# Tokens in halves, split feed-forward chunks and a new order table in a linear-attention and max-out kernel

## The chip, the cores and the metric

The kernel runs on one core of one Trainium2 chip. The metric is the device time of one execution in microseconds. A core has five engines with queues of their own: TensorE (PE; PEld is its weight load), VectorE (DVE), ScalarE (ACT), GpSimd (POOL) and SyncE (SP), which here only issues transfers. Engines work their queues in order and wait for each other by semaphores.

## The reference

q, k and v have shape 8 x 8 x 576 x 64 (batch, heads, tokens, channels), all inputs are float32.

```python
def phi(x):
    proj = np.einsum('bhsd,df->bhsf', x, w_phi)                       # 128 features
    proj = proj - np.max(np.abs(proj), axis=-1, keepdims=True)
    return np.concatenate([np.exp(proj), np.exp(-proj)], axis=-1)
q_p, k_p = phi(q), phi(k)
kv = np.einsum('bhsf,bhsd->bhfd', k_p, v)
z = np.sum(k_p, axis=2)
num = np.einsum('bhsf,bhfd->bhsd', q_p, kv)
den = np.einsum('bhsf,bhf->bhs', q_p, z)[..., None] + 1e-06
x = (num / den).transpose(0, 2, 1, 3).reshape(B * S, H * D)           # 4608 x 512
h = np.maximum(np.maximum(x @ w1, x @ w2), x @ w3)                    # 4608 x 768
out = h @ w_out                                                       # 4608 x 512
```

## The kernel before

The attention runs in 16 units of four heads (unit u is half of batch u // 2). A unit has 18 tiles of 128 tokens: 16 for the first 512 tokens of its four heads and two for the last 64 tokens of each (its tail, which for q is loaded apart, L383). The steps of a unit, with the names that the tables show:

- load q, k, v (`q_raw`, `k_raw`, `v_raw`; for units 0 to 3 q and k are cast on the way by POOL's transfers, L451 and L466, except unit 0's k, L458, which is cast by L462; the tail of q is cast by L487). Casts of later units are on POOL (L510).
- transpose q and k to `qkT`: by PE for units 0 to 3 (L495, copied out by L500), by a transposing transfer for the others (L514).
- project with `w_phi` (L536), take the largest absolute value of each token on DVE (`mk`, `mq`, L548), exponentiate on ACT (`Ek` L545, `Eq` L613 after a second projection L607), scale v by `em` on POOL (`vab`, L566), and multiply into `kvps` (L587), copied to `kv_sb` (L593).
- the quotient: `psn` (L638) holds the two products with exp(proj) and exp(-proj); DVE forms y = psn[0] * sq (L641, the first sums), adds psn[1] (L644) and takes the reciprocal of the denominator (L646); POOL or DVE multiplies (`x_sb`, L648). Each of these works on one or two heads with five tiles of 65 columns.
- transpose to `xT`: by PE for units 0 to 5 (L658, copied by L661), by a transposing transfer for the others (L665).

Every two units make a batch, and its first 512 tokens a feed-forward chunk; the last 64 tokens of all eight batches make a ninth, chunk 8. The maximum over three products is rewritten: w2 and w3 have w1 subtracted (L763, on POOL and DVE), so a chunk needs only x(w2-w1) and x(w3-w1) (`ups`, L688), ReLU (`hT`, L696 or L698), a maximum (L694), and the product with w_out (L721) beside x(w1 w_out) (L716), whose weights are made once (`pwT` L775, `pm` L789). The results are copied out (`osb`, L729) and stored (L736). The weights are loaded by four transfers on POOL (L421).

The order of the work on every engine is written out by hand: `PLAN` is a table of entries such as `1176G@10.0` (node 1176, on POOL, with the time for which it was planned). `plan` reads it and gives each node its engine, its buffers and its place; the engines then run their instructions in the table's order. The eight banks of PSUM and the work buffers are given out in the table too. A `gate` (L479) is a copy of one element on DVE into a `v_raw` buffer, after which that unit's v may be loaded; the load then waits at the head of SP's queue, and all later loads behind it.

Of the kernel before, what the change touches and what calls it, by code (L numbers as in the profile page):

```python
# [8 lines left out]
FP32 = mybir.dt.float32  # L9
# [27 lines left out]
EARLY = 2  # L37
WARM = 28.0
# [46 lines left out]
4G0@0.4 6S0@0.4 2S@1.0 0G@1.2 5G@1.8 8S@2.2 93G1@2.7 10S0@2.8 92G@3.5 7D@3.7 11S0@4.1 3D@4.2 13T0@4.3 253G2@4.3  # L85
14D0@5.0 252G@5.2 9A@5.3 24T001200@5.8 19T34@6.0 27D@6.3 21A@6.5 12G@6.6 15T5@6.7 96G@6.8 23D@6.9 26A@7.0 17T6@7.2
178S0@7.2 16D@7.5 20A@7.5 177G0@7.5 25A@8.0 18D@8.1 29T70@8.2 22D@8.3 176G@8.4 39T35@8.5 63T6200@8.6 30A@8.7 28D@8.9
65A@9.2 1173G@9.2 94D@9.5 42D@9.6 34T41@9.7 31A@9.7 95S@9.8 33D@10.0 1176G@10.0 41A@10.2 36A@10.5 43D@10.6 101T7@10.7
1174G@10.8 32D@10.9 40A@10.9 99T3@11.1 64A@11.2 97T5@11.5 102D1@11.5 1175G@11.6 67A@11.7 37D@11.7 68T0@12.1 58T67@12.2
401S0@12.2 44A0@12.2 98D@12.3 66A@12.4 46G0@12.5 69A@12.9 100D@13.0 108T112511@13.1 35A@13.2 38D@13.6 62A@13.6  # L90
113T31@13.8 256G@13.9 181G@14.1 70A@14.1 112D@14.2 45G@14.3 48A@14.4 103T40@14.6 109A@14.6 117D@14.8 257T2@14.9
104A@15.1 111D@15.4 261T3@15.6 61A@15.6 329S0@15.6 47G@15.7 49G@15.9 262D2@16.0 105A@16.1 107D@16.2 52T073@16.4
59A@16.5 106D@16.8 110A@17.0 50G@17.2 116D@17.4 60A@17.5 118T45@17.7 259T0@18.0 53A@18.0 122D@18.1 128A1@18.2
114A@18.4 123T67@18.5 51G@18.6 121D@18.7 400S@18.8 130G1@18.8 54A@18.9 152T411@18.9 115A@19.1 126D@19.4 154A@19.6
127D@19.7 55T31@19.7 124A@19.9 260D@20.0 119A@20.1 129G@20.1 182T6@20.4 56A@20.6 258D@20.7 125A@20.8 186T0@20.9
71A0@21.1 147T37@21.3 187D0@21.3 132A@21.3 57D@21.5 153A@21.5 72T20@21.6 135G@21.7 183D@21.7 120A@21.8 131G@21.9
75T14@22.0 133G@22.2 149A@22.3 73D0@22.3 184T5@22.4 76D@22.8 155A1@22.8 328S@22.9 151A@23.0 136T162@23.0 74D@23.2
148A@23.4 134G@23.5 77D@23.6 83T10@23.7 150A@23.9 138D@24.0 142T34@24.2 185D@24.2 137A@24.4 80T27@24.6 145A@24.6
# [194 lines left out]
def kernel(  # L293
# [562 lines left out]
```

## Time and profile before

| what | value |
|---|---|
| median of 3 runs | 294.62 us (292.95 to 296.05) |
| the profiled execution | 292.23 us, with a span of 290.1 us |
| PE busy | 270.6 us, 93% of the span, 3502 matmuls |
| DVE busy | 230.2 us, 79%, 458 instructions |
| ACT busy | 204.7 us, 71%, 493 instructions |
| POOL busy | 157.7 us, 54%, 163 instructions |
| moved by transfers | 49.92 MB in 70662 packets, mean 172 GB/s |

The span runs from the first to the last profiled instruction; the rest of an execution's time lies around it. Busy time is the time in which an instruction of the engine is under way. Successive matmuls overlap, so that their mean duration is longer than the distance between them, which a run of them back to back shows.

### The profile page before, as it was taken

To read this page: it belongs to the slowest core of one execution; us is meant where nothing else is said; L and a number is where in the kernel's file an instruction comes from. 1 tells how busy PE (TensorE), PEld (TensorE's weight loads), DVE (VectorE), ACT (ScalarE), POOL (GpSimd) and SP (SyncE) were. 2 spreads that over 40 slices of the span, in tenths; PEclk is the share of its full clock that TensorE was granted. 3 is DMA by queue.
4 is the path that set the end of the run, shared out by engine and by line. 5 is a ranking of instruction groups with operands and counts; after the bars stand their busy time and mean duration, and the time that the engine had idled before them with its cause. 6 is when DMAs were issued, how large, how long until landed. Compare 5 with 4: busy or idle time off the path is not lost.

```text
span 290.1 us, 8572 instructions
## 1 busy us (share of the span) xinstructions
PE 270.6 (93%) x3502; PEld 151.3 (52%) x3502; DVE 230.2 (79%) x458; ACT 204.7 (71%) x493; POOL 157.7 (54%) x163
## 2 busy tenths in 40 slices
PE   1589997899999999998999999999999999999994
PEld 1367643456546645663565445655465555444442
DVE  2699886989998889998999988999999785264430
ACT  2699985789998899689864899999969681210001
POOL 7397659557678636576866396660758533100000
PEclk9998999999999999999999999999999999999999
DMA  7999998793897962799987899627084212100065
GB/s 141 226 280 215 262 259 198 207 273 119 299 279 158 244 192 46 182 321 282 254 245 198 209 333 206 127 21 217 5 129 139 90 37 62 66 3 2 0 217 145
DMA packets 70662, 49.92 MB, mean 172 GB/s; under 512 B 47072, under 2 KB 58720, under 8 KB 70624
## 3 DMA queue, kind: packets, MB, share of 16 engines
q1 hardware_dynamic: 65232, 44.25, 58.7%
q0 software_dynamic: 5312, 5.08, 10.7%
q8 instruction: 27, 0.44, 0.6%
q14 instruction: 11, 0.09, 0.1%
q10 hardware_dynamic: 80, 0.07, 0.1%
HBM read 34.67 MB, written 9.44 MB: 152 GB/s over the span
## 4 chain that ended last, share of the span: by engine, by line
PE 74%; DMA 15%; DVE 6%; issue 1%; POOL 1%; SPq 1%; DVEq 0%; POOLq 0%
PE ups L688 31%; PE ops L721 14%; DMA w_bf<-in_moe_w_dram 11%; PE ops L716 10%; PE psn L638 6%; PE kvps L587 5%; PE psq L536 4%; PE psm L607 3%; DMA q_raw<-in_q_dram 2%; DMA xT<-x_sb 2%; DVE w_bf L763 1%; DVE x_sb L648 1%; DVE y L644 1%; PE pxT L658 1%; PE psk L536 1%
## 5 line engine op out<-in xcount | busy, mean ns | idle before, releaser
L688 PE MATMUL ups<-xT,w_bf 128*128 128x512 bf16 x432 | 99.5, 379 | 4.2 <-DVE w_bf L763 1.4
L545 ACT ACTIVATE Ek<-psk 128x512 bf16<-128x512 f32 (+1 forms) x160 | 83.6, 572 | 12.9 <-PE psk L536 6.7
L566 POOL TENSOR_TENSOR vab<-v_raw,em 128x1152 bf16<-128x1152 f32 (+1 forms) x36 | 69.5, 1950 | 35.8 <-ACT em L558 35.8
L613 ACT ACTIVATE Eq<-psm 128x512 bf16<-128x512 f32 (+1 forms) x160 | 81.9, 588 | 3.1 <-PE psm L607 1.9
L688 PEld LDWEIGHTS <-w_bf 128*128 128x128 bf16 x432 | 39.9, 98 | 52.6 <-issue 4.4
L548 DVE TENSOR_REDUCE mk<-psk 128x4 f32<-128x512 f32 (+1 forms) x80 | 48.7, 630 | 4.7 <-PE psk L536 3.2
L721 PE MATMUL ops<-wout_bf,hT 128*128 128x512 bf16 (+1 forms) x222 | 51.7, 373 | 0.0
L548 DVE TENSOR_REDUCE mq<-psq 128x4 f32<-128x512 f32 (+1 forms) x80 | 48.6, 628 | 2.3 <-PE psk L536 1.3
L696 ACT ACTIVATE hT<-ups 128x512 bf16<-128x512 f32 x36 | 21.8, 611 | 29.0 <-PE ups L688 28.8
L694 DVE TENSOR_TENSOR hT<-hT,ups 128x512 bf16<-128x512 bf16 x54 | 35.2, 678 | 8.3 <-PE ups L688 7.5
L648 POOL TENSOR_TENSOR x_sb<-y,rden 128x640 bf16<-128x640 f32 x22 | 27.4, 1253 | 21.9 <-DVE rden L646 21.0
L641 DVE TENSOR_TENSOR y<-psn,sq 128x325 f32<-128x325 f32 x64 | 29.5, 488 | 6.9 <-PE psn L638 5.0
L721 PEld LDWEIGHTS <-hT 128*128 128x128 bf16 x222 | 20.5, 98 | 21.9 <-issue 0.5
L644 DVE TENSOR_TENSOR y<-y,psn 128x325 f32<-128x325 f32 x64 | 29.4, 488 | 1.4
L638 PEld LDWEIGHTS <-Eq 128*128 128x128 bf16 x640 | 25.0, 97 | 10.3 <-issue 2.5
L729 ACT COPY osb<-ops 128x512 f32<-128x512 f32 (+1 forms) x23 | 13.2, 583 | 23.0 <-PE ops L721 22.7
L638 PE MATMUL psn<-kv_sb,Eq 128*128 128x65 bf16 x640 | 27.5, 194 | 1.3 <-issue 0.4
L536 PE MATMUL psq<-wph,qkT 64*128 64x128 bf16 x288 | 25.9, 224 | 1.2 <-DVE qkT L500 1.0
L536 PEld LDWEIGHTS <-qkT 64*128 64x128 bf16 x576 | 18.6, 97 | 15.8 <-issue 12.0
L536 PE MATMUL psk<-wph,qkT 64*128 64x128 bf16 x288 | 25.4, 224 | 0.3 <-DVE v_raw L479 0.3
L716 PE MATMUL ops<-xT 128*128 128x512 bf16 x96 | 24.6, 380 | 0.0
L587 PE MATMUL kvps<-vab,Ek 64*128 64x65 bf16 x1152 | 22.7, 193 | 0.3 <-ACT Eq L613 0.2
(58 smaller groups left out, 259.9 us busy)
## 6 DMA issues: line engine op xcount, KB each, us to landing
v_raw<-in_v_dram SPq DMA_DIRECT2D x16, 576.0 KB, 7.2
out_dram<-osb SPq DMA_DIRECT2D x32, 256.0 KB, 3.4
k_raw<-in_k_dram SPq DMA_DIRECT2D x12, 576.0 KB, 5.4
q_raw<-in_q_dram SPq DMA_DIRECT2D x12, 512.0 KB, 5.5
w_bf<-in_moe_w_dram POOLq DMA_DIRECT2D x3, 768.0 KB, 25.1
q_raw<-in_q_dram SPq DMA_DIRECT2D x16, 64.0 KB, 5.5
qk_bf<-in_k_dram POOLq DMA_DIRECT2D x3, 288.0 KB, 7.3
qk_bf<-in_q_dram POOLq DMA_DIRECT2D x3, 256.0 KB, 9.9
```

Of the source, the lines that this page charges most:

```text
L536: nc.tensor.matmul(ps()[:, i, :], lhsT=cols[r0:r0 + D, :], rhs=wph[r0:r0 + D, :], start=True, stop=True)
L545: "ek", {"ACT": 0.485 if n == 4 else 0.28}, lambda s=s, t0=t0, n=n, psk=psk: nc.scalar.activation(Ek[s]()[:, t0:t0 + n, :], psk()[:, 0:n, ...
L548: reds.append(nd(kind, {"DVE": 0.607 if n == 4 else 0.34}, lambda ps=ps, m=m, t0=t0, n=n: nc.vector.tensor_reduce(m()[:, t0:t0 + n], ps()[ ...
L566: made.append(any_of(n_, lambda n_, g=g, t0=t0, t1=t1: (nc.vector if n_.eng == "DVE" else nc.gpsimd).tensor_tensor(vab()[:, g, t0:t1, 0:D] ...
L587: nc.tensor.matmul(kvps[ab]()[:, pr, g, :], lhsT=Ek[g]()[r, t, :], rhs=vab()[r, g, t, :], start=(pr == prs[0] and g + j == 0), stop=(pr == ...
L613: "eq", {"ACT": 0.485 if n == 4 else 0.28}, lambda s=s, t0=t0, n=n, psm=psm: nc.scalar.activation(Eq[s]()[:, t0 * P:(t0 + n) * P], psm()[: ...
L638: nc.tensor.matmul(psn[g]()[:, c, :], lhsT=Eq[g]()[:, t0:t0 + P], rhs=kv()[:, pr, ab, g, :], start=True, stop=True)
L644: sums.append(nd("xw", {"DVE": 0.42}, lambda ab=ab, psn=psn, y=y: nc.vector.tensor_tensor(y()[:, ab], y()[:, ab], psn[1](), ALU.add), [n_] ...
L688: nc.tensor.matmul(ups(), lhsT=w_bf[i + 1][:, ct, j * P:(j + 1) * P], rhs=tokens_of(ct), start=(ct == 0), stop=(ct == CT - 1))
L694: nc.vector.tensor_tensor(hT()[:, j, :], hT()[:, j, :], ups(), ALU.max)
L716: nc.tensor.matmul(ops_()[:, 0:width], lhsT=tile_of(ct, tt), rhs=line_w[c_i > MOVE][:, ct, cols], start=(ct == 0), stop=False)
L721: nc.tensor.matmul(ops_()[:, 0:width], lhsT=hT()[:, j, tt * P:(tt + 1) * P], rhs=wout_bf[:, j, cols], start=False, stop=(j == JT - 1))
```

## The change

q's tiles are taken in the order of the halves of the tokens (`tile_of_q`): the transposes of units 0 to 3 pick them so, and for the other units POOL casts each eight tiles of q as two times four. A pass of the quotient now covers one half of the first 512 tokens, two tiles of each head, or three with the tail in the second half, for two heads at a time. A first sum goes to DVE or to ACT, which does it in one instruction per tile with the scale taken from `sq`; the table gives 23 of 64 to ACT. The transposes to `xT` are by PE for units 14 and 15 too, and go by halves. Chunks 0 and 7 become two of 256 tokens each, and the last chunk two of 384 and 128. The table is new from its first to its last entry, with 1690 nodes for 1572. Among other things it puts the tail of q ahead of k on SP's queue, the last weight load behind unit 0's multiplies by v on POOL, and the loads of q and k of units 4 and 5 behind the gate of unit 2's v. The numbers given with the tail's load describe it for the planner and issue nothing.

```diff
+SOON = (0, 1, 14, 15)
+SPLIT = (0, 7)
...
+    def tile_of_q(t):
+        pr, half, ab, c = t // 8, t // 4 % 2, t // 2 % 2, t % 2
+        return 8 * pr + 4 * ab + 2 * half + c if t < MT else t
...
-                           pipe=0.6, hold=-2.0, lat=2.5 if by_pe else 1.7, dmas=2, packet=18.0)
+                           pipe=1.44, lat=1.7, dmas=2, packet=45.0)
...
-                            nc.tensor.transpose(tps()[r:r + D, n, :], qk()[:, c, t0 + n, :], ident)
+                            nc.tensor.transpose(tps()[r:r + D, n, :], qk()[:, c, t0 + n if c else tile_of_q(t0 + n), :], ident)
...
+                    for half in range(2):
+                        copy_on[n_.eng](
+                            qk()[:, t0 + 4 * half:t0 + 4 * half + 4, col:col + D].rearrange("p (a j) d -> p a j d", a=2),
+                            raw_part(u, c, t0, t0 + 8).rearrange("p (a h j) d -> p a h j d", a=2, h=2)[:, :, half])
...
-        for pr in range(2):
-            y = buf("y", 2, [P, 2, 5, W], FP32)
...
+        for half in range(2):
+            nt = 2 + half
+            y = buf("y", 2, [P, 2, 2, 3, W], FP32)
...
-                n_ = nd("xu", {"DVE": 0.42}, lambda pr=pr, ab=ab, psn=psn, y=y: nc.vector.tensor_tensor(
-                    y()[:, ab], psn[0](), sq()[:, 2 * pr + ab, :].unsqueeze(2).to_broadcast([P, 5, W]), ALU.mult),
+                n_ = nd("xu", {"DVE": 0.07 + 0.14 * nt, "ACT": 0.22 * nt}, None, [a, n_sq], [psn[0], sq, y], locks=[psn[0]])
+
+                def scaled(n_, pr=pr, half=half, nt=nt, psn=psn, y=y):
+                    if n_.eng == "DVE":
+                        nc.vector.tensor_tensor(y()[:, pr, :, 0:nt, :], psn[0]()[:, :, 0:nt, :],
+                                                sq()[:, pr, half, :, 0:nt].unsqueeze(3).to_broadcast([P, 2, nt, W]), ALU.mult)
+                        return
+                    for ab in range(2):
+                        for c in range(nt):
+                            nc.scalar.mul(y()[:, pr, ab, c, :], psn[0]()[:, ab, c, :], sq()[:, pr, half, ab, c:c + 1])
...
+            for prs in ([[0], [1]] if u in SOON else [[0, 1]]):
...
-        if u < X_PE:
+            if u < X_PE or u in SOON:
+                pxT = bank("pxT", [P, 2, nt, P], BF16)
...
-    def chunk(c_i, ready, tokens_of, tile_of, out_rows, n_out):
-        hT = buf("hT", 2, [P, JT, SM], BF16)
+    def chunk(c_i, ready, col0, n, tokens_of, tile_of, out_rows, n_out, hT):
+        cols_h = slice(col0, col0 + n)
...
-                ups = bank("ups", [P, SM])
+                ups = bank("ups", [P, n])
...
+        for c0, n in ([(0, 256), (256, 256)] if b in SPLIT else [(0, SM)]):
+            ready = [x for u in (2 * b, 2 * b + 1) for half in range(2) if 256 * half < c0 + n and c0 < 256 * half + 256
+                     for x in units[u]["done"][half]]
...
-    chunk(B, lasts, lambda ct: xT[:, :, ct, SM:SM + ST],
+    for b0, b1 in ((0, 6), (6, 8)):
+        chunk(B, lasts[b0:b1], b0 * ST, (b1 - b0) * ST, lambda ct, b0=b0, b1=b1: xT[:, b0:b1, ct, SM:SM + ST],
```

More of the change, by code (lines that the diff above doesn't have):

```diff
@@ L651, in attention @@
[L651 to L663 removed]
+        divs, done = [], []
@@ L664, in xdma @@
+        if not done:
             def xdma():
@@ L704, in chunk @@
                     evac.append(e)
[L705 removed]
+        for tt in range(col0 // P, (col0 + n) // P):
             halves = 2 if c_i == B and tt == SM // P - 1 else 1
```

451 lines of the change are left out of this document (239 added, 212 removed).

## The prediction

> **What bounds the kernel now.** I read the page first: the span, the busy shares and the shares of the chain that ended last.
>
> ```profile
> span 290.1 us, 8572 instructions
> ...
> PE 270.6 (93%) x3502; PEld 151.3 (52%) x3502; DVE 230.2 (79%) x458; ACT 204.7 (71%) x493; POOL 157.7 (54%) x163
> ...
> PE 74%; DMA 15%; DVE 6%; issue 1%; POOL 1%; SPq 1%; DVEq 0%; POOLq 0%
> ```
>
> PE (TensorE) carries three quarters of the chain and transfers most of the rest. Where each of them stands is told by the table of windows (stretch, its length, then busy us of PE, PEld, DVE, ACT, POOL, granted clock, DMA share, GB/s).
>
> ```profile
> core 0: us, PE busy (x) PEld busy (x) DVE busy (x) ACT busy (x) POOL busy (x), PEclk, DMA share, GB/s
> 0.00:10.00 10.00, 3.10 (x48) 2.42 (x48) 3.58 (x6) 3.72 (x6) 5.29 (x12) 1.00 0.82 155
> 10.00:20.00 10.00, 7.26 (x109) 4.84 (x109) 7.43 (x16) 7.61 (x21) 8.08 (x14) 1.00 1.23 266
> 30.00:40.00 10.00, 9.29 (x131) 6.28 (x126) 8.71 (x26) 9.24 (x18) 4.73 (x7) 1.00 1.14 256
> 40.00:50.00 10.00, 7.72 (x51) 3.07 (x49) 6.88 (x11) 7.01 (x16) 9.38 (x7) 1.00 0.95 234
> 50.00:60.00 10.00, 9.01 (x139) 4.94 (x139) 9.87 (x17) 7.72 (x18) 5.00 (x4) 1.00 0.75 191
> 120.00:140.00 20.00, 19.09 (x254) 10.24 (x253) 18.09 (x39) 16.40 (x40) 15.23 (x15) 1.00 1.11 276
> 240.00:250.00 10.00, 10.00 (x59) 4.70 (x56) 4.26 (x9) 0.59 (x1) 3.38 (x5) 1.00 0.22 61
> ...
> 57.00:286.20 229.20, 227.53 (x2871) 124.23 (x2865) 186.32 (x368) 162.47 (x396) 117.56 (x112) 1.00 0.63 160
> ```
>
> From 57 us to its last matmul PE idles for 1.67 us of 229.2, and at 240 to 250 us not at all, though DVE and ACT are nearly free there. So an order that only fills the end better can bring nothing: PE is full there. What can be had lies in the first 57 us. The chain and the timelines of the queues say what is late there (start, us, what; in brackets the engine's idle time before it).
>
> ```profile
> 0.74 0.40 SPq L458 DMA_DIRECT2D k_raw<-in_k_dram  x1
> 3.06 1.31 SPq L383 DMA_DIRECT2D q_raw<-in_q_dram  x2
> 3.75 7.16 DMA q_raw<-in_q_dram
> 11.04 0.53 POOL L487 CAST qk_bf<-q_raw 128x128 bf16<-128x128 f32 x2 [4.63 <-DMA q_raw<-in_q_dram]
> 11.38 0.42 PE L495 MATMUL tps<-ident,qk_bf 128*64 128x128 bf16 x4 [2.22 <-POOL qk_bf L487]
> 15.43 1.53 POOL L421 DMA_DIRECT2D w_bf<-in_moe_w_dram  x2
> 16.17 30.79 DMA w_bf<-in_moe_w_dram
> 40.62 4.20 POOL L763 TENSOR_TENSOR w_bf<-w_bf 128x1024 bf16<-128x1024 bf16 x2 [3.42 <-DMA w_bf<-in_moe_w_dram]
> 42.79 1.90 PE L688 MATMUL ups<-xT,w_bf 128*128 128x512 bf16 x8 [0.71 <-POOL w_bf L763]
> 47.05 1.05 DVE L763 TENSOR_TENSOR w_bf<-w_bf 128x1024 bf16<-128x1024 bf16 x1 [2.52 <-DMA w_bf<-in_moe_w_dram]
> 48.16 1.90 PE L688 MATMUL ups<-xT,w_bf 128*128 128x512 bf16 x8 [1.39 <-DVE w_bf L763]
> ```
>
> Two late transfers. The 64 tokens that q has beyond 512 (its tail) are issued behind k and w_phi and land at 10.9; the cast on POOL waits 4.63 us, PE 2.22 us, and behind that cast stand, in POOL's queue, unit 2's loads and all four weight loads. So the last weights go out at 16.17, land at 47, and the subtractions on POOL and DVE that feed the first feed-forward matmuls (L688) start at 40.6 and 47.05.
>
> **The change, part by part.** *Start.* q's tail now stands first on SP's queue, ahead of k's two loads, which move by its 1.31 us of issues. It should land near the shortest of its kind and not after 7.16 us.
>
> ```profile
> DMA to landing us min/median/max: 2.7/5.5/9.4
> ...
> 3.59 0.46 DVE L462 CAST qk_bf<-k_raw 128x576 bf16<-128x576 f32 x1 [3.59 <-DMA k_raw<-in_k_dram]
> 5.28 1.06 PE L495 MATMUL tps<-ident,qk_bf 128*64 128x128 bf16 x16 [5.28 <-DMA qk_bf<-in_q_dram]
> 7.00 0.67 ACT L462 CAST qk_bf<-k_raw 128x576 bf16<-128x576 f32 x1 [4.98 <-DMA k_raw<-in_k_dram]
> ```
>
> (The first row is that of line 383, q's tail.) PE's 2.22 us wait for it goes. But both k casts are now on ACT: k's first half lands at 3.6 + 1.3 = 4.9, is cast by 5.6, or some 1 us later where the tail's packets hold it up, against 5.28 for q: the first transposes move by 0.3 to 1.3 us. Gain 2.2 less about 0.7, so 1.5; bounds 0 and 2.2.
>
> *Weights.* The first weight load is no longer behind a stuck cast; the third is still behind unit 3's loads, which need unit 0's buffer; the fourth has been put behind unit 0's four v multiplies on POOL. The q and k loads of units 4 and 5 (four of 0.5 MB, with their tails), which now share the transfers with the weights, come behind the gate of unit 2's v, that is behind unit 1's sums on DVE.
>
> ```profile
> 21.18 0.82 SPq L378 DMA_DIRECT2D q_raw<-in_q_dram  x1
> ...
> DMA to landing us min/median/max: 14.2/22.5/30.8
> ```
>
> (The last row is that of line 421, the weights.) Weights land at 13.9 + 14.2 = 28.1 first and at 47.0 last: 6.3 us for each of three, 4.7 MB of reads beside some 2.8 MB of q, k and v. With most of these gone, 3 x 6.3 x 4.7/7.5 = 12 us is the estimate, so the last is in place near 41, 6 us earlier, and the third near 36. Then it isn't the weights that are last but POOL and DVE, which have unit 1's sums ahead of the subtractions. PE's visible idle time from 40 to 60 us is 2.28 + 0.99 = 3.27 us. I take it all, as 3.3; bounds 1.5 (the subtractions come only 2 us earlier, since POOL and DVE are then full) and 4.0 (with the 0.71 of 30 to 40). Splitting chunk 0 into two of 256 tokens lets its first half start without the second; it is how PE finds work there and has no price of its own beside the next part.
>
> *PE.* The order of instructions shows 20 more transposes of x (60 to 80) and 576 feed-forward matmuls in the place of 432, with the same columns in all.
>
> ```profile
> 60.18 0.62 PE psn L638 x20
> 72.36 0.28 PE pxT L658 x5
> 248.16 16.40 PE ups L688 x76
> ```
>
> A transpose takes 56 ns: +1.1 us. A matmul of 512 columns takes 216 ns, 0.42 ns a column, and one of 65 columns with its own weight load 31 ns, 4 ns more than its columns: 144 more matmuls cost 0.6 us. Sum +1.7; bounds 1.1 (columns alone) and 2.9 (12 ns for each more).
> TensorE: Matmul & The Clock Gate, section Back-to-back issue gap, in the Trainium skill, has 81 ns for a sustained matmul of 128 columns and 131 ns for one of 512; by its 81 ns the 20 transposes and the 48 matmuls of 128 columns would add some 1.8 us more. The trace disagrees on both counts, with 56 and 216 ns.
>
> *First sums.* 23 of 64 first sums (y = psn x sq, L641) go from DVE to ACT, each as 4 or 6 instructions of 65 columns, 118 in all with a scale per partition, which no instruction of the old kernel has.
>
> ```profile
> L641 DVE TENSOR_TENSOR y<-psn,sq 128x325 f32<-128x325 f32 x64 | 29.5, 488 | 6.9 <-PE psn L638 5.0 <-ACT em L558 0.9 <-DVE x_sb L648 0.5
> L545 ACT ACTIVATE Ek<-psk 128x512 bf16<-128x512 f32 x128 | 73.1, 615 | 8.2 <-PE psk L536 5.9 <-DVE mk L548 2.0
> L545 ACT ACTIVATE Ek<-psk 128x256 bf16<-128x256 f32 x32 | 12.4, 401 | 4.7 <-DVE mk L548 3.7 <-PE psk L536 0.8
> L558 ACT ACTIVATE em<-mk 128x18 f32<-128x18 f32 x28 | 4.7, 222 | 2.0 <-DVE mk L548 1.9
> 61.07 0.32 ACT L558 ACTIVATE em<-mk 128x18 f32<-128x18 f32 x2 [1.03 <-DVE mk L548]
> 20.00:120.00 100.00, 95.69 (x1414) 56.06 (x1413) 89.30 (x182) 88.96 (x217) 65.37 (x64) 0.98 0.85 210
> ```
>
> DVE keeps 63% of these columns and saves 10.9 us, but has 55 more instructions of other kinds (492 for 460, and 23 gone), at 0.2 us each of fixed time as much again: even. On ACT two of 18 columns take 0.32 us and one 0.22, a step of 0.10; 512 against 256 columns give 0.84 ns a column; so 65 columns step at 0.10 + 0.04 = 0.14 if the scale costs nothing, at 0.26 (0.22 + 0.04) if nothing overlaps. Units 0 to 7 hold 50 of the 118, and from 20 to 120 us ACT idles for 11.0 us, 5.3 of which (2.99 + 2.28 at 40 to 60) lie in the wait for weights, so 5.8 are free. 50 x 0.14 = 7.0: 1.2 us more than fits. I take +1.2 as the nearest row has it; bounds 0 (at 0.10) and 7.4 (at 0.26). After 120 us ACT has room.
>
> *The rest.* sq's layout, q's order in the transposes and POOL's casts in halves change no path: POOL is idle for 46% of the span, and PE's 1.67 us of idle time after 57 us is what a late cast would add to. Ordering the tokens by halves and splitting chunk 7 and the last chunk feeds a PE that is full; I cost it at nothing, and its loss is a rival below. The waits in the middle, such as the 0.91 us at 120 to 140, may go: not counted, bound -1.6.
>
> The sum: -1.5 - 3.3 + 1.7 + 1.2 = -1.9 us, so a span of 288.2. The profiled execution took 292.23 us, 2.1 beside its span, and would take 290.3. It is 2.4 us below the median of the runs, 294.62; from that median the forecast is 292.7 us.
>
> **Rivals.** *ACT becomes the bound (slower).* Place: units 0 to 7, where ACT frees the banks that PE refills. It decides from a step of 0.12 us, where 50 steps pass the 5.8 us; at 0.26 they are 7.4 us over, and the end is -1.9 - 1.2 + 7.4 = +4.3: 298.9 us. For it: ACT is busy for 89 of 100 us there. Against: the small activations step at 0.10.
> ScalarE: Activation LUTs, section What ACT_TABLE_LOAD costs, in the Trainium skill, gives 93 ns more for each operand read per partition; by its figures a step would be an estimated 0.24 us and the end +3.1. No run here shows such an operand yet.
> *All of it comes.* Start 2.2, weights 4.0, middle 1.6, PE +1.1, ACT 0: -6.7, or 287.9 us. For it: every one of these waits is in the rows above.
> *The weights are no bound for PE.* If DVE, 9.87 us busy of 10 at 50 to 60, is next at once, the 3.3 is lost: +1.4, 296.0 us.
> *The last halves are exposed.*
>
> ```profile
> L648 POOL TENSOR_TENSOR x_sb<-y,rden 128x640 bf16<-128x640 f32 x22 | 27.4, 1253 | 21.9 <-DVE rden L646 21.0 <-PE psn L638 0.8
> L646 DVE RECIPROCAL rden<-y 128x10 f32<-128x10 f32 x32 | 6.2, 208 | 0.3
> ```
>
> Units 14 and 15 now finish later, beside chunk 6; if their last sums have no cover, PE waits once for two sums of 0.49, a reciprocal of 0.21, a multiply of up to 1.25 and the transposes' copy, near 0.5: 3 us, in all +1.1, 295.7 us. Against: chunk 6's down products and part of the last chunk's stand between them in PE's order.
>
> **How the numbers follow.** Forecast 0.48, all of it 0.18, ACT 0.17, weights 0.09, exposed halves 0.08. A measurement of this kernel can tell about 1%, 2.9 us. The forecast's own range, from the bounds of start, weights and PE with ACT up to 2.5, is -4.5 to +0.5, 290.1 to 295.1 us; about a third of it is faster by over 1%. Faster: 0.17 + 0.18 = 0.35. Slower: 0.17 and 0.03 from the two that end near +1.2: 0.20. Same: 0.45. The range leaves the better half of "all of it" and the worse half of ACT's case out: 288.5 to 298.0.
>
> **What would show it.** Right: the second group of transposes at L495's place has no wait for a q cast; the first DVE subtraction of weights starts before 43 us; PE idles under 2 us from 40 to 60; the 65-column activations step at 0.10 to 0.16 us; PE from 60 us to its end idles under 3 us. Wrong: steps near 0.25 with PE waiting for ACT before 130 us; PE idle beyond 240 us on copies of xT; weights still landing after 44 us.

## The result and the profile after

The changed kernel is slower: 306.48 us (median of 4 runs, 306.0 to 307.69) against 293.78 us for the kernel before in the same session; the ratio is 1.0466 (95% interval 1.0412 to 1.0519). The forecast was 292.7 us, no change to speak of, so it missed the sign as well as the range. The profiled execution took 306.75 us with a span of 305.0, against 292.23 and 290.1.

First the page of the changed kernel: its span, busy shares and the chain that ended last, by engine.

```profile
span 305.0 us, 9082 instructions
PE 273.4 (90%) x3623; PEld 164.4 (54%) x3666; DVE 242.2 (79%) x490; ACT 227.6 (75%) x621; POOL 160.5 (53%) x208
PE 63%; DVE 13%; ACT 13%; DMA 4%; issue 3%; POOL 1%; SPq 1%; DVEq 0%; ACTq 0%
```

TensorE's share of the chain (the work that ended last, followed back) fell from 74% to 63%; VectorE rose from 6% to 13%, and ScalarE, which had none, has 13%. The kernel before was full on one engine; this one hands over between three. 43 matmul records are missing in this trace (3623 matmuls for 3666 weight loads). A second execution of the same order (the run a2 below) has all of them, so the table of windows is shown from it, the kernel before first and the changed order second (stretch, length, busy us of PE, PEld, DVE, ACT, POOL, granted clock, DMA share, GB/s).

```profile
0.00:60.00 60.00, 46.06 (x719) 29.04 (x720) 46.32 (x95) 45.18 (x106) 40.14 (x51) 0.97 1.01 222
60.00:240.00 180.00, 178.35 (x2555) 100.41 (x2554) 164.13 (x333) 152.90 (x376) 114.19 (x107) 1.00 0.73 184
240.00:290.10 50.10, 46.18 (x235) 21.85 (x231) 19.73 (x33) 6.57 (x12) 3.38 (x5) 1.00 0.24 70
```

```profile
0.00:60.00 60.00, 43.09 (x645) 30.37 (x647) 44.43 (x91) 44.43 (x118) 41.60 (x58) 0.97 0.79 171
60.00:240.00 180.00, 174.31 (x2417) 98.61 (x2411) 158.46 (x311) 160.04 (x440) 106.55 (x139) 1.00 0.77 193
240.00:306.10 66.10, 60.49 (x616) 37.12 (x614) 39.51 (x91) 23.39 (x63) 12.36 (x12) 0.99 0.21 66
```

The account of the 16.0 us between these two spans (306.1 - 290.1): PE idles 3.0 us more before 60 us (60 - 43.09 against 60 - 46.06), 4.0 us more from 60 to 240 (5.69 against 1.65), 1.7 us more after that (5.61 against 3.92), and it is busy for 7.3 us more (277.9 against 270.6). So about two thirds of the visible idle time (5.7 of 8.7 us) lies behind 60 us, where the prediction expected none.

What happened at the start is seen in the changed kernel's chain (first row) and in the timelines of ACT, PE and DVE.

```profile
3.88 6.14 DMA wphi_f<-in_w_phi_dram
7.22 0.67 ACT L480 CAST qk_bf<-k_raw 128x576 bf16<-128x576 f32 x1 [5.20 <-DMA k_raw<-in_k_dram]
7.94 1.17 PE L513 MATMUL tps<-ident,qk_bf 128*64 128x128 bf16 x16 [1.24 <-ACT qk_bf L480]
10.11 0.23 DVE L435 CAST wph<-wphi_f 128x128 bf16<-128x128 f32 x1 [0.38 <-DMA wphi_f<-in_w_phi_dram]
10.40 0.28 PE L565 MATMUL psq<-wph,qkT 64*128 64x128 bf16 x1 [0.40 <-DVE v_raw L497]
```

The tail's two loads stand ahead of k on SP, so the first half of k lands at 7.19 us instead of 3.56, ACT casts it until 7.9, and the first group of transposes ends at 9.11 instead of 6.34. The tail's two loads and k's two stand ahead of w_phi, which lands at 10.02 instead of 5.16; DVE casts it at 10.11, and the first projection begins at 10.40. In the kernel before it began at 7.14. Of these 3.3 us the transposes, late through k, make up 2.8; w_phi is what came last, and holds the projection for the rest.

And what became of the weights, from the timelines of POOL, DVE and PE:

```profile
40.92 6.60 POOL L812 TENSOR_TENSOR w_bf<-w_bf 128x1024 bf16<-128x1024 bf16 x3
48.56 3.20 DVE L812 TENSOR_TENSOR w_bf<-w_bf 128x1024 bf16<-128x1024 bf16 x2
48.98 4.76 POOL L595 TENSOR_TENSOR vab<-v_raw,em 128x1152 bf16<-128x1152 f32 x2 [1.46 <-issue]
51.82 2.46 DVE L812 TENSOR_TENSOR w_bf<-w_bf 128x1024 bf16<-128x1024 bf16 x1
54.67 3.76 PE L737 MATMUL ups<-xT,w_bf 128*128 128x256 bf16 x20 [3.24 <-DVE mk L577]
```

The last weights landed at 37.03 us, not 46.96. But the subtractions did not begin earlier: POOL's began at 40.92 (40.62 before) and DVE's at 48.56 (47.05 before), both without a wait for weights, behind other work in their queues. Of DVE's three the first took 0.68 us; the other two ran beside POOL's multiplies into vab and took 2.60 and 2.46 us. The maximum (mk) behind them in DVE's queue was late, and PE stood still for 3.24 us. The wait for weights went and a wait of the same length took its place.

The groups behind the first sums and the quotient, in the changed kernel, and last the row of x's multiplies on DVE before:

```profile
L682 ACT ACTIVATE y<-psn,sq 128x65 f32<-128x65 f32 x118 | 26.5, 348 | 6.9 <-PE psn L669 6.6
L684 DVE TENSOR_TENSOR y<-y,psn 128x260 f32<-128x260 f32 (+1 forms) x64 | 30.3, 489 | 13.9 <-ACT y L682 10.9 <-PE psn L669 0.7 <-DVE y L677 0.5
L696 DVE TENSOR_TENSOR x_sb<-y,rden 128x256 bf16<-128x256 f32 (+1 forms) x27 | 24.5, 922 | 0.2
L812 DVE TENSOR_TENSOR w_bf<-w_bf 128x1024 bf16<-128x1024 bf16 x3 | 5.7, 1912 | 0.0
L648 DVE TENSOR_TENSOR x_sb<-y,rden 128x640 bf16<-128x640 f32 x10 | 10.4, 1039 | 0.2
```

DVE's second sums wait 10.9 us for ScalarE. The new table gives DVE 27 of 64 multiplies of x, where the old one gave it 10 of 32: 24.5 us of busy time for 10.4. They average 922 ns and the weight subtractions 1912 ns, each a mean over short and very long ones (408 to 2166 ns, and 675 to 2602).

### The profile page after: what moved, and what is told of

It is laid out like the page before. It is cut to its first block, busy times and chain, and to the rows that moved or that the text cites. A ratio compares the mean times of both kernels' runs of the same rounds, so it can differ in the third digit from the quotient of the medians.

```text
span 305.0 us, 9082 instructions
## 1 busy us (share of the span) xinstructions
PE 273.4 (90%) x3623; PEld 164.4 (54%) x3666; DVE 242.2 (79%) x490; ACT 227.6 (75%) x621; POOL 160.5 (53%) x208
## 4 chain that ended last, share of the span: by engine, by line
PE 63%; DVE 13%; ACT 13%; DMA 4%; issue 3%; POOL 1%; SPq 1%; DVEq 0%; ACTq 0%
PE ups L737 29%; PE ops L770 9%; ACT y L682 7%; PE ops L765 7%; PE kvps L616 5%; PE psq L565 4%; PE psn L669 4%; DVE x_sb L696 3%; ACT Ek L574 3%; PE psm L636 3%; DMA out_dram<-osb 2%; ACT Eq L642 2%; DMA wphi_f<-in_w_phi_dram 2%; DVE y L684 2%; DVE w_bf L812 2%
## 5 line engine op out<-in xcount | busy, mean ns | idle before, releaser
L737 PE MATMUL ups<-xT,w_bf 128*128 128x512 bf16 (+3 forms) x560 | 102.2, 328 | 5.1 <-DVE mk L577 3.2
L642 ACT ACTIVATE Eq<-psm 128x512 bf16<-128x512 f32 (+1 forms) x160 | 84.4, 597 | 12.4 <-PE psm L636 12.3
L574 ACT ACTIVATE Ek<-psk 128x512 bf16<-128x512 f32 (+1 forms) x160 | 86.9, 592 | 7.2 <-PE psk L565 5.1
L737 PEld LDWEIGHTS <-w_bf 128*128 128x128 bf16 x576 | 52.6, 99 | 44.1 <-DVE mk L577 3.4
L696 POOL TENSOR_TENSOR x_sb<-y,rden 128x384 bf16<-128x384 f32 (+1 forms) x37 | 28.0, 767 | 41.5 <-DVE rden L690 36.6
L743 DVE TENSOR_TENSOR hT<-hT,ups 128x512 bf16<-128x512 bf16 (+3 forms) x72 | 37.2, 546 | 10.5 <-PE ups L737 8.1
L684 DVE TENSOR_TENSOR y<-y,psn 128x260 f32<-128x260 f32 (+1 forms) x64 | 30.3, 489 | 13.9 <-ACT y L682 10.9
L745 ACT ACTIVATE hT<-ups 128x512 bf16<-128x512 f32 (+3 forms) x46 | 22.6, 521 | 15.2 <-PE ups L737 14.4
L669 PEld LDWEIGHTS <-Eq 128*128 128x128 bf16 x640 | 26.1, 98 | 12.8 <-issue 4.1
L682 ACT ACTIVATE y<-psn,sq 128x65 f32<-128x65 f32 x118 | 26.5, 348 | 6.9 <-PE psn L669 6.6
L696 DVE TENSOR_TENSOR x_sb<-y,rden 128x256 bf16<-128x256 f32 (+1 forms) x27 | 24.5, 922 | 0.2
```

What stands on the lines that cost most here:

```text
L574: "ek", {"ACT": 0.485 if n == 4 else 0.28}, lambda s=s, t0=t0, n=n, psk=psk: nc.scalar.activation(Ek[s]()[:, t0:t0 + n, :], psk()[:, 0:n, ...
L642: "eq", {"ACT": 0.485 if n == 4 else 0.28}, lambda s=s, t0=t0, n=n, psm=psm: nc.scalar.activation(Eq[s]()[:, t0 * P:(t0 + n) * P], psm()[: ...
L669: nc.tensor.matmul(psn[g]()[:, ab, c, :], lhsT=Eq[g]()[:, t0:t0 + P], rhs=kv()[:, pr, ab, g, :], start=True, stop=True)
L682: nc.scalar.mul(y()[:, pr, ab, c, :], psn[0]()[:, ab, c, :], sq()[:, pr, half, ab, c:c + 1])
L696: nc.vector if n_.eng == "DVE" else nc.gpsimd).tensor_tensor(
L737: nc.tensor.matmul(ups(), lhsT=w_bf[i + 1][:, ct, j * P:(j + 1) * P], rhs=tokens_of(ct), start=(ct == 0), stop=(ct == CT - 1))
```

## Experiments: the first sums on ScalarE

Four theories stood against each other: the operand and the handover of ScalarE's first sums; VectorE held up by POOL; the start; and the new order itself. Each ratio below is against the kernel before, measured again in the same session (its medians were 292.3 to 295.3 us). Differences in us to the changed kernel's 306.48 compare sessions, and are good to about 1 us: a2, which is the changed order once more, measured 307.53.

**a1, the 23 first sums back on VectorE, at the same places.**

```diff
-88A1@23.6 173A1@32.9 241A0@51.7 252A@52.1 ...
+88D1@23.6 173D1@32.9 241D0@51.7 252D@52.1 ...
```

> The changed kernel with its 23 first sums given back to DVE, at the same places of the order; nothing else. Theory ACT (an instruction of 65 columns with a scale per partition steps at 0.20 us, so the 118 of them cost 23 us of ACT, and PE waits for it): the time falls by 5 to 9 us, to some 298 to 301 us, and PE's idle time from 60 to 180 us falls with it. Theory DVE (DVE's multiplies beside POOL are what is slow, and DVE is the bound): the time falls by less than 2 us or rises, because DVE takes on 23 sums of 0.34 to 0.48 us, 9 us in all. Theory start (the loss is made before 60 us and carried to the end): within 2 us.

Measured: 303.26 us, ratio 1.0372 (1.0322 to 1.0422). That is 3.2 us of the 12.7 (4.3 against a2, in the same session), below the 5 to 9 that the theory of ScalarE asked for, so the sums are one cause and not the cause.

**a4, the same thing alone in the old order:** 23 first sums of the kernel before on ScalarE, five instructions each.

```diff
-84D1@25.1 165D1@29.2 241D@52.8 ...
+84A1@25.1 165A1@29.2 241A@52.8 ...
...
+                    for c in range(5):
+                        nc.scalar.mul(y()[:, ab, c, :], psn[0]()[:, c, :], sq()[:, 2 * pr + ab, c:c + 1])
```

> The old kernel with 23 of its 64 first sums on ACT, in the same units as in the changed one, five instructions of 65 columns each, 115 in all; the rest of the order is the old one. Theory ACT: slower by 4 to 8 us, 298 to 302 us, with steps of 0.20 us. Theories DVE and start: within 2 us of the old kernel's 293.8.

Measured: 305.07 us, ratio 1.0447 (1.039 to 1.0504), 12.8 us more than before, where the theory asked for 4 to 8. Its groups of the first and the second sums:

```profile
L645 ACT ACTIVATE y<-psn,sq 128x65 f32<-128x65 f32 x115 | 26.9, 380 | 1.3 <-DVE x_sb L651 1.1 <-POOL x_sb L651 0.2
L647 DVE TENSOR_TENSOR y<-y,psn 128x325 f32<-128x325 f32 x64 | 30.0, 490 | 26.4 <-ACT y L645 21.6 <-issue 4.0
```

In an order made for sums on DVE, DVE waits 21.6 us for them; the new table had half of that (10.9). So in the old order this one move costs as much as the whole change does; the two can't be added up.

**a7, the operand alone.** Same count, shapes and places; the scale is a number in the instruction, which leaves out the scale by sq in these 23 parts.

```diff
-nc.scalar.mul(y()[:, pr, ab, c, :], psn[0]()[:, ab, c, :], sq()[:, pr, half, ab, c:c + 1])
+nc.scalar.mul(y()[:, pr, ab, c, :], psn[0]()[:, ab, c, :], 0.5)
```

> The changed kernel with ScalarE's first sums scaled by 0.5 written in the instruction instead of by a value for each partition from sq; this leaves out the scale by sq of those 23 units (their x is not the reference's), and the count, shapes, places and order of all instructions stay. Operand theory: the step from start to start of the 65-column instructions falls from 0.196 us to 0.10 to 0.12, ScalarE is busy 8 to 12 us less, and the time falls by 3 to 6 us. Handover theory (what costs is that VectorE's second sum has to wait for ScalarE behind the tensor engine, whatever ScalarE's step): 0.5 to 2 us. If nothing is gained, neither is the reason.

Measured: 300.69 us, ratio 1.027 (1.0212 to 1.0328), 5.8 us below the changed kernel.

```profile
L682 ACT ACTIVATE y<-psn 128x65 f32<-128x65 f32 x118 | 16.2, 260 | 7.6 <-PE psn L669 6.6 <-DVE x_sb L696 0.9
```

The group's busy time fell by 10.3 us (26.5 to 16.2). The median step from start to start fell from 0.197 to 0.104 us. With a cheap step ScalarE's help is worth having: this is 2.6 us better than a1, which doesn't use it at all. So the operand is what turns ScalarE's help into a loss; what the handover costs is still in the 300.69 us, and is less than the help saves.

**m1, the disputed costs by themselves,** in a small kernel of its own (its lines are shortened here).

```diff
+nc.scalar.mul(ya, psa, sq[:, i:i + 1])              # 24 times, L96
+nc.scalar.activation(ya, psa, ID, scale=0.5)        # 24 times, L98
+nc.scalar.copy(ya, psa)                             # 24 times, L100
+nc.vector.tensor_tensor(x, y, y2 to_broadcast, ALU.mult)   # L84: 12 alone, 24 beside 8 of POOL's
+nc.vector.tensor_tensor(y, y, psn, ALU.add)                # L88: 12 alone, 24 beside 8 of POOL's
+nc.gpsimd.tensor_tensor(vab, vraw, em to_broadcast, ALU.mult)  # L92
```

> A kernel of its own that leaves the whole computation out; it measures the disputed costs by themselves. ScalarE, 24 instructions of 65 columns out of PSUM in each group: step from start to start with the scale from a tile (L96) 0.19 to 0.21 us; with the scale written in the instruction (L98) 0.10 to 0.12; a plain copy (L100) 0.10 to 0.12. If the operand costs nothing, all three are alike. VectorE: a multiply with two inputs in SBUF alone (L84), as x's; the same while POOL multiplies 128x1152 (L92); a sum with one input in PSUM alone (L88) and while POOL multiplies. Contention theory: L92's mean is 2 to 4 times L84's while POOL is busy, and POOL's own multiplies are longer than alone; the sums out of PSUM are not changed by POOL. Otherwise all VectorE means agree within 20%.

ScalarE's timeline (start, duration of the block):

```profile
2.12 5.06 ACT L96 ACTIVATE ya<-psa,sq 128x65 f32<-128x65 f32 x24
6.87 3.06 ACT L98 ACTIVATE ya<-psa 128x65 f32<-128x65 f32 x24
9.63 3.06 ACT L100 COPY ya<-psa 128x65 f32<-128x65 f32 x24
```

From start to start of the blocks that is 4.75/24 = 0.198 us with the operand, and 2.76/24 = 0.115 us without; the copy's 3.06 is the same. The operand costs 83 ns an instruction.

## Experiments: VectorE beside POOL

In m1, the groups of VectorE and POOL while POOL multiplies (12.9 to 31.2 us); then VectorE's blocks of twelve multiplies alone, twelve sums alone, and the sums beside POOL:

```profile
L84 DVE TENSOR_TENSOR x<-y,y 128x256 bf16<-128x256 f32 x9 | 18.2, 2022 | 0.3
L92 POOL TENSOR_TENSOR vab<-vraw,em 128x1152 bf16<-128x1152 f32 x8 | 17.6, 2196 | 13.2 <-DVE em L105 12.6
```

```profile
1.99 5.46 DVE L84 TENSOR_TENSOR x<-y,y 128x256 bf16<-128x256 f32 x12
7.48 5.46 DVE L88 TENSOR_TENSOR y<-y,psn 128x260 f32<-128x260 f32 x12
38.38 10.98 DVE L88 TENSOR_TENSOR y<-y,psn 128x260 f32<-128x260 f32 x24
```

While POOL multiplied, only nine of VectorE's multiplies began, one for each of POOL's eight and the one before them: 2022 ns in the mean, where twelve alone take 5.46 us. The first took 424 ns and the other eight 2220 to 2223, beside POOL's 2175 to 2325. The two engines alternate, and VectorE loses the whole length of POOL's instruction. The sum with an input in PSUM isn't touched: 5.46/12 = 0.455 us alone, 10.98/24 = 0.458 beside POOL. SBUF — State Buffer, section SBUF: two separate sides, in the Trainium skill, says this of a VectorE instruction with two inputs in SBUF: it shares one pair of ports with GpSimd, by a lock for the whole instruction. The run agrees.

**a6, unit 4's casts on POOL ahead of unit 2's multiplies into vab.** (The expectations call unit 4 "chunk 4".)

```diff
-344G1@48.4 345G@49.4 346G@50.0 343G@50.7
+344G1@43.1 345G@43.2 346G@43.3 343G@43.4
```

> The changed kernel with one move on POOL: the four casts of chunk 4 (L532, L535, L539) go ahead of unit 2's two multiplies into vab (L595), so that VectorE's three weight subtractions (L812) run beside casts, or beside an idle POOL, and not beside POOL's multiplies. Contention theory (a VectorE instruction with two inputs in SBUF stands still while POOL multiplies): L812 on VectorE falls from 5.7 us in all to 2.0 to 3.5, the tensor engine's wait of 3.24 us at 51 to 55 us for mk shrinks to under 1, and the whole gains 1.5 to 3 us unless the later vab makes L616 wait (bounded by about 3 us). Without contention (the subtractions are long for another reason, such as cold or late weights): L812 stays at 5 to 6 us, and the end is 0 to 3 us later.

Measured: 305.5 us, ratio 1.0439 (1.0375 to 1.0502). The line of the subtractions (durations min/median/max) and the wait that is now PE's:

```profile
L812 DVE TENSOR_TENSOR w_bf<-w_bf x3: 683/739/886, 48.2 to 49.7; 128x1024 bf16<-128x1024 bf16 x3
PE kvps L616 <- POOL vab L595: 2.4, 2, 1.6
```

The contention is gone, 1912 ns to about 740, and so is PE's wait of 3.24 us; but PE now waits 2.4 us for vab, and the end gains 1.0 us, less than the two intervals can tell apart. That POOL's multiplies hold the subtractions up is shown; as a price of the end it is small here.

**a3, VectorE's 27 multiplies of x on POOL.**

```diff
-181D@37.1 325D1@68.7 336D@69.0 ...
+181G@37.1 325G1@68.7 336G@69.0 ...
```

> The changed kernel with the 27 multiplies of x by 1/den that DVE does (24.5 us of busy time, 922 ns each) given to POOL at the same places of the order. Theory DVE: the time falls by 5 us or more. Theory ACT: it falls by less than 2 us, or rises, since POOL needs 0.77 us for each and its v multiplies come later. Theory start: within 2 us.

Measured: 308.25 us, ratio 1.0554 (1.0502 to 1.0605). That is 0.7 us over a2 in the same session. POOL becomes later than VectorE was: PE's longest wait behind 60 us is now 2.4 us, for an x_sb of POOL. Nothing is to be had in that direction.

**c1, VectorE's multiplies of x by a constant,** which leaves out the division in these 27 parts (lines shortened).

```diff
-nc.vector.tensor_tensor(x_sb, y, rden to_broadcast, ALU.mult)
+nc.vector.tensor_scalar(x_sb, y, 0.5, None, ALU.mult)
```

> The changed kernel with VectorE's 27 multiplies of x (L696) by a constant 0.5 instead of by rden; this leaves out the division in those 27 parts, and leaves VectorE one input in SBUF instead of two. Order, places and counts stay. Contention theory: L696 on VectorE falls from 24.5 us to 7 to 13 us, VectorE is no longer held by POOL, and if this is what held the tensor engine after 60 us, the time falls by 2 to 4 us, to 302.5 to 304.5. Slack theory (VectorE's lost time was idle time anyway, as moving the multiplies to POOL gained nothing): L696 falls as much, and the time by less than 1 us.

Measured: 305.25 us, ratio 1.0434 (1.0386 to 1.0481), 1.2 us below the changed kernel, with overlapping intervals. The edit didn't free VectorE as expected (24.5 us of busy time became 19.3, not 7 to 13). Its group, one such multiply begun under POOL's vab, and two with no POOL instruction beside them:

```profile
L695 DVE TENSOR_SCALAR x_sb<-y 128x256 bf16<-128x256 f32 (+1 forms) x27 | 19.3, 730 | 0.0
155.23 1.64 DVE L695 TENSOR_SCALAR x_sb<-y 128x256 bf16<-128x256 f32 x1
212.63 0.48 DVE L695 TENSOR_SCALAR x_sb<-y 128x256 bf16<-128x256 f32 x2
```

This multiply from SBUF to SBUF with one input is held by POOL as well: 1.64 us against some 0.28; POOL's vab ends at 156.73, and it at 156.87. So this run doesn't price the contention; 5 us less of VectorE's time came with about 1 us, which the intervals can't tell from nothing.

## Experiments: the start

**a5, SP's first loads in the order of the kernel before.**

```diff
-10S0@0.7 6S0@2.0 8S@2.6 2S@3.2
+6S0@0.4 2S@1.0 8S@2.2 10S0@2.8
```

> The changed kernel with SP's first loads in the order of the kernel before: first half of unit 0's k, w_phi, second half of k, then q's tail (in the changed kernel q's tail stands first and w_phi last). Nothing else is touched; the other queues are the same. Start theory (the changed kernel's first projection waits for w_phi, landed 10.0 us, and this is carried to the end because the tensor engine is full later): w_phi lands near 5.5, the first projection L565 starts near 7 to 8 instead of 10.4, and the whole time falls by 2.5 to 4 us, to about 303. Slack theory (later stalls of the changed kernel, above all the 3.2 us at 51 to 55 us, take up whatever the start gives): the first projection is earlier, the end moves by under 1 us. Third possibility: q's tail, now last, holds up the first projection of the tail instead and the start gains nothing.

Measured: 308.88 us, ratio 1.0556 (1.0497 to 1.0615). w_phi was early and the first projection came at 12.04, later than 10.40: VectorE's queue has a cast of the tail first, and PE's has the tail's transposes ahead of the projections, where PE waits 3.9 us. **a2** was meant to put w_phi first by itself. Its entry was moved in the table, but not its time, by which the loads are ordered, so SP's order stayed as it was: a second measurement of the changed order, at 307.53 us, ratio 1.0512 (1.045 to 1.0573).

> The changed kernel with the two w_phi loads moved to the head of SP's queue; nothing else. Theory start: the first projections begin at some 8 us instead of 10.4, and the end comes 2 to 3 us earlier, some 304 us. Theories ACT and DVE: the 2 to 3 us gained at the start are lost again to the engine that is the bound by 60 us; the time stays within 1 us of 306.5.

**a8, three things undone:** sums on VectorE, SP's order as in a5, casts as in a6.

> The changed kernel with three things at once: all 23 first sums on VectorE again (that alone took it to 303.3), SP's first loads in the order of before, and chunk 4's casts ahead of unit 2's vab. If the three costs add (3.2, 2.5 to 4 and 1.5 to 3 us): 297 to 300. If they share one slack: 301 to 303. What is left over the kernel before is then the order itself, with its 2.8 us more of tensor-engine work.

Measured: 303.55 us, ratio 1.0367 (1.0313 to 1.0421), the time of a1 alone. That the casts' gain was spent on the worse start is a reading of a5 and a6, not shown by itself.

**a9, sums on VectorE, w_phi ahead of the tail, and VectorE's subtractions ahead of POOL's.**

```diff
-2S@3.2 1226D@43.5 1227D@44.1 1228D@44.9
+2S@0.1 1226D@34.4 1227D@34.41 1228D@34.42
```

> The changed kernel with all first sums on VectorE (that alone measured 303.3) and two moves: w_phi's loads go ahead of q's tail on SP, q's tail second, and VectorE's three weight subtractions go to where VectorE stands at about 38.5 us, ahead of POOL's own subtractions and multiplies into vab. Contention theory: the subtractions take 2.0 to 3.0 us in all instead of 5.7, the tensor engine's wait of 3.2 us between 51 and 55 us is gone and no later vab takes its place: 2 to 3.2 us less. Start theory in its second form (w_phi ahead of everything, the tail not held back): the first projection begins 1 to 2.5 us before 10.4, 1 to 2.5 us less. Together 298 to 300. If the earlier subtractions only push the rest of unit 1 back, or the start's order only exchanges one late load for another: 302 to 304.

Measured: 303.97 us, ratio 1.0371 (1.0318 to 1.0425). The subtractions took 685 ns each and PE's wait for mk is gone, but k now lands later, PE waits 6.1 us for its cast, and the first projection begins at 13.20:

```profile
11.21 1.61 PE L513 MATMUL tps<-ident,qk_bf 128*64 128x128 bf16 x19 [6.09 <-ACT qk_bf L480]
```

**c2, the whole start of the kernel before** (SP's loads, w_phi's cast first, the tail's cast and transposes behind the first projections), with a1's sums and a9's subtractions.

```diff
-10S0@0.7 6S0@2.0 8S@2.6 2S@3.2 100D@4.0 3D@7.6 17T1@7.7 18D@8.1 39T51@8.5 40A@9.0 43D@9.1
+6S0@0.4 2S@1.0 8S@2.2 10S0@2.8 3D@3.9 17T1@8.72 18D@8.85 39T51@8.9 100D@9.25 40A@9.75 43D@10.2
```

> The changed kernel with first sums on VectorE and the early weight subtractions (as in the run that measured 303.97), and the start of the kernel before in all queues: SP loads k's first half, w_phi, k's second half, then q's tail; VectorE casts w_phi first and the tail after the first projections; the tensor engine makes the first projections ahead of the tail's transposes. Start theory in its third form (not one load, but the tail standing ahead of the first projections on the tensor engine and on VectorE): the first projection begins at 7.0 to 8.5 us instead of 13.2, the time lost by 30 us falls by 2 to 4 us, and the end to 299.5 to 302. If the first data are bound by the loads as a whole, the end stays at 303 to 304.

Measured: 304.97 us, ratio 1.0438 (1.0381 to 1.0495). Its first projection and two of PE's waits before 62 us (from its longest execution, 308.42 us):

```profile
7.76 0.28 PE L565 MATMUL psq<-wph,qkT 64*128 64x128 bf16 x1 [0.79 <-DVE qkT L518]
PE kvps L616 <- POOL vab L595: 4.1, 1, 4.1
PE tps L513 <- POOL qk_bf L505: 2.6, 1, 2.6
```

The first projection is as early as wanted, and PE then waits 2.6 us for the tail and 4.1 us for vab. So three other orders of the start (a5, a9, c2) were tried in the new table, two of them together with other moves, and none beat its own.

**b1, the start step in a mild form in the kernel before:** the tail ahead of k's second half, behind w_phi and k's first.

```diff
-10S0@2.8
+10S0@2.0
```

> The kernel before with one move on SP: q's tail is loaded ahead of the second half of unit 0's k instead of behind it; w_phi stays ahead of it. This is the start step of the prediction by itself: the tensor engine waits 2.2 us at 11.4 us for the cast of the tail. If the tail is what the start waits for, it lands 0.5 to 1.5 us earlier, that wait shrinks to 1 to 1.5 us and the end comes 0.5 to 1.5 us earlier. If the queues share one bandwidth, k's second half comes later by as much and nothing is gained (within 0.5 us).

Measured: 293.09 us, ratio 1.0011 (0.9982 to 1.0039).

```profile
11.90 1.17 PE L495 MATMUL tps<-ident,qk_bf 128*64 128x128 bf16 x17 [3.40 <-ACT qk_bf L462]
```

PE's wait of 2.2 us for the tail is gone, and a wait of 3.4 us for k's cast stands in its place. In this form the start step is worth nothing.

## Experiments: the weights alone, and what is left

**b2, the kernel before with unit 4's two large loads behind unit 3's v** on SP, and unit 4's first cast later on POOL.

```diff
-328S@22.9 327S@26.0 334G2@30.7
+328S@33.0 327S@33.3 334G2@41.5
```

> The kernel before with the two large loads of chunk 4 (q and k, 590 KB) moved on SP behind unit 3's v, and chunk 4's first cast on POOL behind the weight subtractions. This is the weights step of the prediction by itself, in the old order: the weights should land 3 to 6 us before 47.0, and the tensor engine's waits between 40 and 60 us (3.3 us idle) shrink. By the prediction's term: 1.5 to 3 us less. If something else follows at once (chunk 4's data now late, or DVE's own order): within 1 us, or later by up to 2.

Measured: 290.83 us, ratio 0.9937 (0.9908 to 0.9966): 1.9 us faster than before, and the fastest version of the kernel here. The last weights land at 43.55. PE's waits from 40 to 60 us, before (first fence) and here:

```profile
PE ups L688 <- DVE w_bf L763: 1.4, 1, 1.4
PE ups L688 <- DVE mq L548: 0.9, 1, 0.9
PE ups L688 <- POOL w_bf L763: 0.9, 2, 0.7
```

```profile
PE ups L688 <- DVE mq L548: 1.8, 1, 1.8
PE ups L688 <- ACT hT L696: 0.7, 1, 0.7
```

The waits for weights are gone, and a part came back as the wait for mq, behind a subtraction that takes 2.54 us beside POOL.

**b4, b2 with unit 4's last q cast ahead of unit 2's vab on POOL.**

```diff
-332G@48.0
+332G@42.65
```

> The kernel before with chunk 4's large loads later (that measured 0.9937 of it) and, on POOL, chunk 4's last q cast ahead of unit 2's multiplies into vab, so that VectorE's third weight subtraction doesn't run beside POOL's multiply. Contention theory: this subtraction falls from 2.54 us to about 0.7, the tensor engine's wait of 1.8 us for mq at 50 us to under 0.6, and the time by 0.5 to 1.8 us more, to a ratio of 0.988 to 0.992. If the multiply into vab is late instead, or the wait goes to another: 0.992 to 0.997.

Measured: 291.34 us, ratio 0.9956 (0.9929 to 0.9983), not to be told from b2. The longest subtraction fell from 2.54 only to 2.09 us, not to the 0.7 expected, and PE's wait for mq is still 1.5 us.

**c3, c2 with c1's multiplies.**

> The run with first sums on VectorE, early subtractions and the start of before, and VectorE's multiplies of x by a constant (the division left out in those 27). If the costs add: 2 to 4 us below that run, 296 to 299. What then still stands above the kernel before (292.5) is the new order itself: its longer list of tensor-engine work and the waits of its halves. If contention on x costs nothing in the end: within 1 us of that run.

Measured: 302.94 us, ratio 1.034 (1.0292 to 1.0387): 2.0 us below c2, but 10 us over before.

**c4, a7, c1 and a6 at once, with the changed kernel's own start.** The scale by sq and the division stay left out as in those two.

> The changed kernel with three costs out at once and its own start order kept: ScalarE's first sums scaled by a constant in the instruction, VectorE's multiplies of x by a constant (both leave the true scale and division out of those parts), and chunk 4's casts ahead of unit 2's multiplies into vab. Singly these measured 5.8, about 1.2 and 1.0 us under the changed kernel's 306.5. If they add: 298 to 299. If they share one slack with each other: 300 to 301. If they hold one another up (each hides behind the others): below 297. What then still stands above the kernel before (292.5) belongs to the new order itself and its start, which no run took apart.

Measured: 297.15 us, ratio 1.0115 (1.0024 to 1.0207). Singly the three gained 5.8, 1.2 and 1.0 us; together 9.3 (306.48 - 297.15), so they don't share one slack. Its first window (43 matmul records are missing in this trace too, 3 of them here):

```profile
0.00:60.00 60.00, 44.09 (x723) 31.90 (x726) 43.03 (x97) 45.77 (x123) 41.45 (x58) 1.00 0.86 185
```

Without these costs, two of which go only with a part of the arithmetic, the new order is still slower, by 0.2% to 2.1%; the runs of the kernel before that were measured beside it spread from 292.0 to 296.7 us, so the size of the rest is not settled. Up to 60 us PE idles 15.9 us, 2.0 more than before. What in the order makes up this rest wasn't taken apart; that the finer pieces give more handovers is argued, not shown.

## Why the prediction was wrong

The step that failed first is "PE is full", from which everything behind 57 us was put at nothing; with it fell the size of the first sums, "even" for VectorE, and the gains of start and weights. The runs put these in its place, part by part.

- **"PE is full after 57 us", so the rest at nothing: wrong.** It was a statement on the old order. In the new one PE idles 5.7 us from 60 to 240 us instead of 1.65, on many small waits, none over 0.9 us. "Full" was a property of the schedule, not of the work, and the bound of -1.6 had a better side only.
- **First sums, +1.2 (0 to 7.4): mis-sized.** The step was 0.198 us, not 0.14: the operand costs 83 ns. With 0.198 the forecast's own sum gives 50 x 0.198 - 5.8 = 4.1 us for this term. ScalarE: Activation LUTs, section What ACT_TABLE_LOAD costs, in the Trainium skill, has 93 ns for the operand, and m1 agrees within 10 ns. The term measured 3.2 (a1) to 5.8 us (a7), within the bounds but far above the value taken. The forecast took the cheap end because the nearest row (0.10 for two small activations) seemed to bear on it; that row has no such operand.
- **VectorE "even": wrong, and no bound was given.** DVE's busy time rose by 12.0 us (230.2 to 242.2). The sum had 10.9 us saved on first sums, of which 9.8 came (29.5 to 19.7), but it left out that the table moves multiplies of x from POOL to DVE, 14.1 us more, and counted instructions with their durations alone: part of these multiplies and two of three subtractions stood under POOL's instructions. The end's share of it is about 1 us each where it could be tried (a6, c1), and c1 didn't remove all of it.
- **Weights, -3.3 (1.5 to 4.0): the landing right, the gain wrong.** Landing 10 us earlier was better than forecast. The step named POOL and DVE as next, and its worst case still had the subtractions come 2 us earlier; in this table they came 0.3 and 1.5 us later, and beside vab they took 1912 ns each in the mean, not 1168. PE's visible idle time from 40 to 60 us was 4.0 us, not less than 3.27. In the old order the same idea, b2, is worth 1.9 us, inside the bounds. So "the weights are no bound" was the rival that happened here, through DVE's queue as it said; what filled that queue it didn't say.
- **Start, -1.5 (bounds 0 and -2.2): wrong, outside its bounds.** The step had k's first half cast by 5.6 us or some 1 us later; it was cast by 7.9, because k took 5.0 us to land behind the tail instead of 2.8. It also left out w_phi, which the same move put behind four loads. The first projection came 3.3 us later instead of a gain, and by 20 us PE had idled 1.0 us longer (10.6 against 9.6 in the two traces of the table of windows). b1 shows that a mild form of the step gains nothing either (1.0011): the wait moves to k.
- **PE's work, +1.7 (1.1 to 2.9): right, by the steps.** In a2's complete trace the feed-forward matmuls (ups) step at 56, 109, 163 and 216 ns for 128, 256, 384 and 512 columns, so 48, 192, 48 and 288 of them take 0.3 us more than 432 of 512 columns, and 20 transposes at 56 ns add 1.1. PE's busy time grew by 7.3 us all the same. A record lasts longer than its step (379 ns against 216), so short waits are counted as busy, and the other 6 us are read as such waits; this is worked out, not tested by a run.
- **The sum and its range.** The range of -4.5 to +0.5 doesn't follow from the bounds it names: with each at its slow end and ACT at 2.5 they add up to 0 - 1.5 + 2.9 + 2.5 = +3.9 us. Even the slow end of all bounds, with ACT at 7.4, is +8.8 us, and the change cost 12.7.
- **The rivals.** ACT as the bound had the sign; it decided from a step of 0.12 us, which 0.198 passes, and by its own sum that step gives an end of +1.0 us (its +4.3 was for 0.26). The rest came from places for which the sum had gains or zeros. The last halves were exposed in part: PE's visible waits behind 240 us are 1.4 us where there were none, for sums of ACT and DVE, under half of the 3 us priced.
- **The signs.** One of the five for "right" came: the second group of transposes had no wait for a q cast. DVE's first subtraction began at 48.56 us and not before 43, PE idled 4.0 us from 40 to 60, the activations stepped at 0.198 us, and from 60 us to its last matmul PE idled 7.1 us, not under 3.

## What to carry to other kernels

When a table reorders everything, an engine that was full stays full only if every hand-over behind it still arrives in time, so a schedule's slack must be priced anew at each stage and with a bound on the slow side. For each load that is moved ahead, list the ones it moves back, and ask which of them the first useful matmul needs. Price an instruction by rows with the same kind of operands, and a VectorE instruction from SBUF to SBUF by what POOL runs beside it.

## What was not expected of the hardware

PE's wait of 3.24 us cost more than itself in the changed kernel. Its windows behind the wait (first two rows), those of a7 with PE's row there, and two of the kernel before:

```profile
54.00:56.00 2.00, 1.33 (x7) 0.95 (x8) 1.81 (x4) 0.00 (x0) 2.00 (x5) 0.54 0.00 0
56.00:58.00 2.00, 2.00 (x13) 1.49 (x12) 0.75 (x2) 0.55 (x2) 2.00 (x7) 0.60 0.00 0
```

```profile
54.00:56.00 2.00, 1.38 (x13) 1.25 (x14) 2.00 (x5) 0.00 (x0) 2.00 (x5) 1.00 0.00 0
56.00:58.00 2.00, 2.00 (x65) 1.61 (x64) 1.88 (x7) 1.50 (x4) 2.00 (x7) 1.00 0.00 0
54.62 2.36 PE L737 MATMUL ups<-xT,w_bf 128*128 128x256 bf16 x20 [3.23 <-DVE mk L577]
```

```profile
20.00:22.00 2.00, 1.71 (x45) 1.26 (x45) 2.00 (x5) 2.00 (x5) 2.00 (x3) 0.69 1.20 270
22.00:24.00 2.00, 2.00 (x32) 1.38 (x31) 1.86 (x4) 1.91 (x7) 1.40 (x4) 0.50 1.17 206
```

The granted clock fell to 0.54 and 0.60 for some 4 us, and the next 20 matmuls of 256 columns took 3.76 us. In a7's trace the same wait was 3.23 us, the clock stayed at 1.00, and the same 20 took 2.36 us: the fall costs 1.4 us. The traces of a1, a2, a3, a5 and c1 have this wait too (3.2 to 3.7 us), and the clock fell behind it in all five. But the kernel before has such a fall at 20 to 24 us, where no wait in the 9 us ahead of it is longer than 0.5 us. TensorE: Matmul & The Clock Gate, section What's actually happening, in the Trainium skill, has the clock halved after an idle window of about 3.4 us. The traces agree on the half; that such a window sets off each fall they don't show. A wait of this length can be dearer than the profile's column of idle time says.
